# A fused recurrence and two-matmul kernel on one core: w's row on another queue, the columns' step earlier, three loads and four small steps reordered

## The chip, the cores and the metric

The kernel runs on one core of a Trainium2 chip. A core has five engines that run their own instruction streams and meet at semaphores: TensorE (PE, matrix products, with PEld for its weight loads), VectorE (DVE), ScalarE (ACT), GpSimd (POOL) and SyncE (SP, which here only issues transfers). Transfers between HBM and the on-chip memory run on 16 DMA engines that all queues share. The metric is the device time of one execution in microseconds (us); lower is better.

## The reference

There are two parts in a row. The first is a linear attention with a decayed state, for 4 batches, 8 heads, 768 tokens and a head size of 48:

```python
for t in range(S):
    cur = einsum('bhd,bhe->bhde', u[None] * kt, vt)
    y[:, :, t] = einsum('bhd,bhde->bhe', rt, state + cur)
    state = w[None, :, :, None] * state + einsum('bhd,bhe->bhde', kt, vt)
```

The second takes the 3072 tokens with 384 features each, and computes `h = x @ w_in` (384 x 2048), `g = max(0.01 * h, h)` and `g @ w_out` (2048 x 384). All inputs and the output are f32; inside, most operands are bf16.

## The kernel before

**Stages.** The 768 tokens of a batch are cut into 6 chunks of 128 tokens, so there are 24 stages: stage n is one chunk of one batch, and stages 0 to 3 are the first chunks of the four batches. Within a chunk the recurrence is turned into matrix products. Rows of r and k are scaled with powers of w around the chunk's middle (tables `qtab`, `ktab`), turned so that the head features lie on the partitions (`tp`), and multiplied to a 128 x 128 matrix per head, which is masked to its triangle (`at`) and multiplied with v. From stage 4 on the state from the chunk before is added (`st`). The result, turned, is `xT`. The second part takes it in groups of four stages: `w_in` products into `gT` (ScalarE applies the leaky step), then `w_out` products into `out_sb`.

**The order.** A text, `ORDER`, lists all steps by short names, and `run` (L844) goes through it. Each name adds instructions to one engine's stream. A step waits only for what it reads or overwrites (`Sched.add`, L72), but every engine works through its own steps strictly in the order of the text; a DMA is issued by the engine on which it is added, in its place in that stream. The eight PSUM banks are handed out in the order of the text as well (`take`, `give`).

**The names that matter here** (a number behind a name is the stage; q and k, or a and b, are halves):

- `w8`, `w`, `u8`, `u`: four small loads of w and u. `w8` brings w with heads on partitions, `w` brings its row (`w_row`, L807). `k0`, `r0` load stage 0 in f32, on the queues of ScalarE and SyncE (L249). `k1`, `r1`, `v1` and so on load 96 KB each (as bf16), `wi0` to `wi3` a quarter of `w_in`, `wo0` to `wo3` a quarter of `w_out`; all of these are issued by GpSimd (L268, L278, L282).
- `qk0`, `v0z`, `v0y`, `wlz`, `zr`: VectorE writes zeros into gaps of tiles. `v0z` does it for v of stages 0 to 3, `v0y` for stages 4 to 23 (L354, L815); `zr` also fills a gap of `w_head` (L359). `one`, `ones`, `id8`, `id`, `tri`, `exps` are constants that VectorE makes; `trow`, `tcol` are GpSimd's.
- `Cw` (L618): w into columns, on TensorE; `Wl` its logarithm, `E` the table for stage 0's turned tiles, `bc` w spread over partitions, `lnw` its logarithm, `qtab`, `ktab` the tables (L393), `W` the state's decay `wl` (L657).
- `wu8` (L403), `Cu` (L629), `C` (L645): the product w u into the two columns `wu`. `u16`, `U` (L409), `utab`: u spread over partitions.
- `c0q@`, `c0k@` (L485): stage 0's r and k as bf16 into `raw`. `P` (L437) scales r or k of a stage on VectorE, `T` (L491) turns it on TensorE, `t` (L507) copies it out; `X` (L452) is `prod`, the product q k of a stage 0 to 3, `D` (L578) its sums on TensorE, `Q` scales v with them (L459); from stage 4 on `q` is row sums on VectorE (L466 to L470) and `Q` a product on GpSimd (L477). `A` (L521) is the matrix product, `M` the mask (L559, L563), `Y` (L692) the sum into PSUM, `y` its copy, `K` and `S` the state (L604, L677).
- `G`, `J` the products with `w_in` (L758), `g`, `j` their copies (L769); `H`, `h` those with `w_out` (L782, L794). `F2`, `F4` are 2 or 4 matmuls on constants with no use for the result (L315).

The first of GpSimd's loads are issued in this order: r1, wi1, k1, k3, v3, v0, r3, v1, r2, k2, wi3, k5, r5, r4, wi2, v2, k4, v4, wi0, v5, wo3.

Of the kernel before, what the change touches and what calls it, by code (L numbers as in the profile page):

```python
# [6 lines left out]
ALU = mybir.AluOpType  # L7
AF = mybir.ActivationFunctionType
# [4 lines left out]
B, H, S, D = 4, 8, 768, 48  # L13
# [3 lines left out]
NST = B * NC  # L17
HD = H * D
E = 64
NP = H // 2  # L20
# [4 lines left out]
NB = B  # L25
TURNED, DIAG, CARRY, EXACT, RAW = 6, 4, 4, 1, 1
STRIPS = 8
SWAP = 12
ORDER = """
w8 qk0 k0 v0z one r0 trow ones v0y tcol wlz r1 id8 wi1 u8 zr table Cw Wl id E w bc lnw c0q@ T0q c0k@ tri u exps k1 T0k  # L30
u16 wu8 Cu t0q t0k qtab P1q F2 k3 v3 U A0 ktab T1q v0 t1q X0 C D0 P1k T1k t1k F4 M0b P3k M0a T3k K3 utab X1 A1 D1 Q0
Y0 t3k P0k r3 P3q v1 M1a T3q r2 y0 k2 K0 M1b Q1 P2q W G0.1 Y1 t3q X3 wi3 A3 y1 g0.1 S3 T2q D3 G1.1 g1.1 k5 t2q r5 r4
P2k T2k wi2 S0 v2 M3b t2k Q3 G0.3 g0.3 G1.3 k4 M3a Y3 P5k A2 y3 P4q T4q v4 wi0 T5k v5 wo3 t4q g1.3 G3.1 q5 t5k Q5 G3.3
g3.3 P5q r6 wo2 X2 g3.1 M2b wo1 G3.2 D2 Q2 G0.2 g0.2 T5q t5q K2 P4k T4k M2a t4k S2 G1.2 g3.2 q4 Q4 K1 S1 Y2 A5 A4 G1.0
y2 G2.1 M5a G0.0 G2.3 M4a M5b Y5 g0.0 y5 M4b Y4 y4 G2.2 g2.2 K4 J2.4 j2.4 k6 wo0 J2.1 J2.2 g1.0 g1.2 S4 k7 P6q q6 j2.1
P6k P7k G2.0 r7 q7 X6T J2.6 j2.6 J2.3 j2.3 k8 G3.0 J2.7 j2.7 k9 r9 j2.2 J2.5 P7q g3.0 g2.3 X7T J2.0 H1 h1 r8 g2.0 Q6
P9k j2.0 H0 j2.5 H3 Q7 P9q X9T A6 P8k q8 P8q X8T v6 A7 M6a v7 M7a g2.1 ts qtabs ktabs H2 h2 v9 v11 v10 M6b Y6 M7b tris
y6 Q8 Y7 y7 K5 r11 K6 S6 r10 k10 S5 v8 k11 k12 k14 K7 S7 q9 Q9 h0 h3 J3.0 j3.0 J3.1 j3.1 J3.2 j3.2 J3.3 j3.3 J3.4 j3.4
J3.5 j3.5 J3.6 j3.6 J3.7 j3.7 A8 A9 M8a M8b M9a M9b P10q P10k X10T P11q P11k X11T r12 r14 k13 r13 q10 Q10 q11 Q11 H4
h4 Y8 Y9 y8 y9 K8 K9 S8 S9 P12q P12k X12T P13q P13k X13T s8 s9 H5 h5 J4.0 j4.0 J4.1 j4.1 J4.2 j4.2 J4.3 j4.3 J4.4 j4.4  # L40
J4.5 j4.5 J4.6 j4.6 J4.7 j4.7 q12 q13 A10 A11 M10a M10b M11a M11b v12 v14 k15 r15 v13 v15 Q12 Q13 H6 h6 H7 h7 Y10 Y11
y10 y11 K10 K11 B6 M12a M12b M13a M13b S10 S11 P14q P14k X14T P15q P15k X15T s10 s11 q14 q15 J5.0 j5.0 J5.1 j5.1 k16
k18 r16 r18 k17 r17 Q14 Q15 J5.2 j5.2 J5.3 j5.3 J5.4 j5.4 J5.5 j5.5 J5.6 j5.6 J5.7 j5.7 H8 h8 H9 h9 Y12 Y13 y12 y13
K12 K13 B7 M14a M14b M15a M15b S12 S13 P16q P16k X16T P17q P17k X17T s12 s13 q16 q17 J6.0 j6.0 J6.1 j6.1 v16 v18 k19
r19 v17 v19 Q16 Q17 J6.2 j6.2 J6.3 j6.3 J6.4 j6.4 J6.5 j6.5 J6.6 j6.6 J6.7 j6.7 H10 h10 H11 h11 Y14 Y15 y14 y15 K14
K15 B8 M16a M16b M17a M17b S14 S15 P18q P18k X18T P19q P19k X19T s14 s15 q18 q19 J7.0 j7.0 J7.1 j7.1 k20 k22 r20 r22
k21 r21 Q18 Q19 J7.2 j7.2 J7.3 j7.3 J7.4 j7.4 J7.5 j7.5 J7.6 j7.6 J7.7 j7.7 H12 h12 H13 h13 Y16 Y17 y16 y17 K16 K17 B9
M18a M18b M19a M19b S16 S17 P20q P20k X20T P21q P21k X21T s16 s17 q20 q21 J8.0 j8.0 J8.1 j8.1 v20 v22 k23 r23 v21 v23
Q20 Q21 J8.2 j8.2 J8.3 j8.3 J8.4 j8.4 J8.5 j8.5 J8.6 j8.6 J8.7 j8.7 H14 h14 H15 h15 Y18 Y19 y18 y19 K18 K19 B10 M20a
M20b M21a M21b S18 S19 P22q P22k X22T P23q P23k X23T s18 s19 q22 q23 J9.0 j9.0 J9.1 j9.1 Q22 Q23 J9.2 j9.2 J9.3 j9.3  # L50
J9.4 j9.4 J9.5 j9.5 J9.6 j9.6 J9.7 j9.7 H16 h16 H17 h17 Y20 Y21 y20 y21 B11 M22a M22b M23a M23b J10.0 j10.0 J10.1
j10.1 J10.2 j10.2 J10.3 j10.3 J10.4 j10.4 J10.5 j10.5 J10.6 j10.6 J10.7 j10.7 H18 h18 Y22 Y23 y22 y23 H19 h19 J11.0
j11.0 J11.1 j11.1 J11.2 j11.2 J11.3 j11.3 J11.4 j11.4 J11.5 j11.5 J11.6 j11.6 J11.7 j11.7 H20 h20 H21 h21 H22 h22
"""


# [6 lines left out]
class Sched:  # L63
# [7 lines left out]

    def add(self, eng, emit, R=(), W=(), dma=None):  # L72
        o = Op()
        o.eng, o.emit, o.dma, o.inc, o.val = eng, emit, dma, False, None
        deps = []
        for key in R:
            w = self.writer.get(key)
            if w is not None:
                deps.append((w, True))
        for key in W:  # L80
            w = self.writer.get(key)
            if w is not None:
# [63 lines left out]
def bass_rwkv5_eagle__then__act_leaky_relu_kernel(  # L146
# [13 lines left out]
    def SB(name, shape, dt=BF16):  # L160
        return ctx.enter_context(nc.sbuf_tensor(name, shape, dt))
# [30 lines left out]
    ones = SB("ones", [128, 128])  # L192
# [10 lines left out]
    qk = [SB(f"qk{i}", [128, 2 * H, E]) for i in range(NQK)]  # L203
# [47 lines left out]
    def load_one(n, which, pace=()):  # L251
# [6 lines left out]
        if swapped(n):  # L258
# [5 lines left out]
            dst = both.rearrange("p n (h e) -> p (n h) e", h=H)[:, :, 0:D]  # L264
            add("pool", lambda: G.dma_start(dst, src), R=pace, W=[(which, n0, half), (which, n0 + 2, half)],
                dma=f"{which}{n}")
            return
        add("pool", lambda: G.dma_start(dst, src), R=pace, W=[(which, n)], dma=f"{which}{n}")  # L268

# [40 lines left out]
    def fill(n):  # L310
# [7 lines left out]

        add("pe", emit, R=["ones"], W=[("ps", i), f"fill{n}"])

# [32 lines left out]
    def zero_v(n0, n1):  # L353
        add("dve", lambda: V.memset(v_sb[:, n0:n1, :].rearrange("p n (h e) -> p (n h) e", e=E)[:, :, D:E], 0.0),  # L354
            W=[("v0", n) for n in range(n0, n1)])
# [66 lines left out]
    def hd(x):  # L422
        return x.rearrange("p (h d) -> p h d", d=D)

    def k_of(n):
        return k_sb[:, slot(n), :] if n >= EXACT else k_f[:, n, :]

    def r_of(n):
        return r_sb[:, slot(n), :] if n >= EXACT else r_f[:, n, :]

    def prep_half(n, half):
        iq = n % NQK
        src, tab, name, done = ((r_of(n), qtab, "r", "qp"), (k_of(n), ktab, "k", "kp"))[half]
        named = "qk"[half] + "tab"
        if swapped(n):
            tab, named = (qtab_s, ktab_s)[half], named + "_s"
        add("dve", lambda: V.tensor_tensor(qk[iq][:, H * half:H * half + H, 0:D], hd(src), hd(tab[:, :]), ALU.mult),  # L437
            R=loaded(name, n) + [named, ("qk0", iq)], W=[(done, iq)])

    def turn_dma(n):  # L440
        iq = n % NQK
# [203 lines left out]
    def decay_columns():  # L645
        ps_c, key = c_bank["u"]
        for hh in range(2):
            rows = slice(64 * hh, 64 * hh + D)
            add("dve", lambda rows=rows, hh=hh: V.tensor_copy(
                wu[rows, :, hh:hh + 1].rearrange("p m o -> p (m o)"), ps_c[rows, 0:NP]),  # L650
                R=[key, "wu"], W=[f"wu{hh}"])
        give(key)

# [134 lines left out]
    def g2_out(n, c0=0, c1=HD):  # L788
# [7 lines left out]
        if swapped(n):  # L796
# [7 lines left out]

    half_of = {"q": 0, "k": 1, "a": 0, "b": 1}
    single = {
        "w": lambda: add("sp", lambda: SP.dma_start(  # L807
            w_row[0:65:64, :], dram(w, 0, [[HD // 2, 2], [1, HD // 2]])),
            W=["w_row"], dma="w"),
        "w8": lambda: add("sp", lambda: SP.dma_start(w_head[:, :, 0:D], twice(w)), W=["w_head"], dma="w8"),  # L810
# [1 line left out]
        "u": lambda: add("sp", lambda: SP.dma_start(u_row[:, :], row(u)), W=["u_row"], dma="u"),  # L812
        "one": lambda: add("dve", lambda: V.memset(one_row[:, :], 1.0), W=["one_row"]),
        "tcol": tokens, "trow": token_rows, "ones": filled, "exps": exponents, "v0z": lambda: zero_v(0, NB),
        "v0y": lambda: zero_v(NB, NST), "zr": zero_raw, "qk0": zero_qk, "wlz": zero_w,  # L815
        "id": identity, "tri": triangle, "table": preload, "id8": small_identity, "wu8": wu_product,
        "bc": spread_w, "lnw": log_w, "qtab": lambda: table(qtab, tcol, "q", "tcol"),
        "ktab": lambda: table(ktab, kexp, "k", "kexp"), "Cw": w_columns, "Cu": wu_columns, "E": turned_table,
# [94 lines left out]
```

## Time and profile before

| | |
|---|---|
| median of 3 runs | 167.31 us (166.94 to 167.38) |
| the profiled execution | 166.78 us |
| its span, first to last instruction | 165.0 us |
| busy in the span | PE 157.4, PEld 119.7, DVE 105.5, ACT 90.4, POOL 109.5 us |
| transfers | 20.21 MB, 123 GB/s in the mean |

A profile is of one execution. Its times are microseconds from the span's start. In a timeline a row has the start, the length, the engine, the line, the operation with its tiles (out<-in), the number of instructions that the row merges, and in brackets how long the engine was idle before it and what ended the wait. In the chain of waits a row has the start, the length and what the end of the kernel waited for. In the view of transfers a row ends with the size and the median time from the start of an issue to the landing. In the table by stretches the columns are the stretch, its length, the busy time of PE, PEld, DVE, ACT and POOL, the granted clock, the DMA engines' share and GB/s. An "ACTq" or "SPq" is the engine's sequencer, which issues and waits. Matmuls are pipelined and their ends are modelled, so a busy PE isn't always PE at its peak.

### The profile page before, as it was taken

How to read it: one execution, taken by the hardware profiler on the slowest of the kernel's cores; microseconds unless marked ns; L12 is line 12 of the kernel's file. 1: busy time of each engine (PE TensorE's matmuls, PEld its weight loads, DVE VectorE, ACT ScalarE, POOL GpSimd, SP SyncE). 2: the span in 40 equal slices, each digit the busy share in tenths (PEclk: the TensorE clock that was granted, in tenths of full speed). 3: DMA queues.
4: the chain of work that ended last, by engine and by line, in shares of the span. 5: the costliest groups of instructions: out<-in, count | busy, mean ns of one | idle time of the engine just before them, and what ended most of it. 6: DMA issues, size and time to landing. Idle time of an engine off the chain costs nothing.

```text
span 165.0 us, 5331 instructions
## 1 busy us (share of the span) xinstructions
PE 157.4 (95%) x2303; PEld 119.7 (73%) x2303; DVE 105.5 (64%) x254; ACT 90.4 (55%) x170; POOL 109.5 (66%) x125
## 2 busy tenths in 40 slices
PE   0899999999999999999999999999999999999994
PEld 0487899985568678668668678678678668678663
DVE  7798998269378699948939939939939933000000
ACT  3856883865168339347447447438438439449121
POOL 8999798987999969999199399299380270000000
PEclk9999999999999999999999999999999999999999
DMA  7999999999999999999939959959980630020023
GB/s 110 149 141 158 169 189 190 181 150 154 149 153 202 121 118 137 158 208 130 160 90 113 145 134 94 163 132 81 104 192 4 127 97 3 4 61 34 17 82 97
DMA packets 101365, 20.21 MB, mean 123 GB/s; under 512 B 94555, under 2 KB 101342, under 8 KB 101342
## 3 DMA queue, kind: packets, MB, share of 16 engines
q0 software_dynamic: 76512, 10.03, 93.2%
q1 hardware_dynamic: 23790, 9.65, 29.8%
q8 instruction: 18, 0.29, 0.8%
q10 hardware_dynamic: 1040, 0.20, 0.6%
q14 instruction: 5, 0.04, 0.1%
HBM read 20.45 MB, written 4.72 MB: 153 GB/s over the span
## 4 chain that ended last, share of the span: by engine, by line
PE 91%; ACT 2%; DVE 2%; DMA 2%; SPq 1%; issue 0%; ACTq 0%
PE ps L782 38%; PE ps L758 37%; PE ps L719 6%; PE ps L529 2%; PE ps L500 2%; DMA w_row<-in_w_dram 2%; PE ps L548 1%; PE ps L595 1%; PE ps L604 1%; PE ps L315 1%; ACT xT L733 1%; DVE at L559 1%; PE ps L379 1%; DVE st L677 1%; PE ps L712 1%; ACT out_sb L794 0%
## 5 line engine op out<-in xcount | busy, mean ns | idle before, releaser
L758 PE MATMUL ps<-xT,w_in_sb 128*128 128x256 bf16 (+1 forms) x672 | 66.2, 257 | 0.2
L782 PE MATMUL ps<-w_out_sb,gT 128*128 128x384 bf16 (+2 forms) x400 | 64.6, 320 | 0.0
L769 ACT ACTIVATE gT<-ps 128x512 bf16<-128x512 f32 x96 | 56.3, 598 | 14.8 <-PE ps L758 10.9
L758 PEld LDWEIGHTS ps<-xT,w_in_sb 128*128 128x128 bf16 x672 | 57.2, 98 | 6.6 <-ACT xT L733 0.5
L477 POOL TENSOR_TENSOR at<-ident,s_tok 128x512 bf16<-128x512 bf16 x40 | 42.1, 1081 | 24.8 <-DVE s_tok L470 24.7
L782 PEld LDWEIGHTS ps<-w_out_sb,gT 128*128 128x128 bf16 x400 | 38.1, 98 | 23.1
L794 ACT ACTIVATE out_sb<-ps 128x384 f32<-128x384 f32 (+2 forms) x25 | 11.8, 478 | 45.3 <-PE ps L782 45.3
L563 DVE CAST_PREDICATED at<-mask,ps 128x512 bf16<-128x512 uint16 x28 | 17.8, 685 | 4.7 <-PE ps L529 4.6
L563 DVE CAST_PREDICATED at<-mask_s,ps 128x512 bf16<-128x512 uint16 x12 | 7.7, 687 | 16.1 <-PE ps L548 16.1
L268 POOL DMA_DIRECT2D v_sb<-in_v_dram x18 | 16.3, 920 | 0.0
L268 POOL DMA_DIRECT2D r_sb<-in_r_dram x17 | 15.7, 928 | 0.1
L268 POOL DMA_DIRECT2D k_sb<-in_k_dram x17 | 15.6, 924 | 0.0
L468 DVE TENSOR_TENSOR rku<-r_sb,ku 128x384 bf16<-128x384 bf16 x20 | 12.2, 611 | 0.7
L733 ACT ACTIVATE xT<-ps 128x384 bf16<-128x384 f32 x24 | 10.8, 491 | 2.7 <-PE ps L719 2.6
L470 DVE TENSOR_REDUCE s_tok<-rku 128x8 f32<-128x384 bf16 x20 | 11.1, 553 | 0.7
L719 PE MATMUL ps<-at,v_sb 128*32 128x128 bf16 x384 | 10.8, 223 | 0.0
L719 PEld LDWEIGHTS ps<-tp,st 128*32 128x32 bf16 x240 | 7.2, 96 | 3.0 <-issue 2.9
L719 PEld LDWEIGHTS ps<-at,v_sb 128*32 128x32 bf16 x384 | 8.8, 98 | 0.5 <-issue 0.2
L719 PE MATMUL ps<-tp,st 128*32 128x128 bf16 x240 | 9.1, 221 | 0.0
L671 DVE TENSOR_TENSOR sum_t<-ps,st 64x192 bf16<-64x192 f32 x24 | 8.5, 354 | 0.6
L466 DVE TENSOR_TENSOR ku<-k_sb,u_tab 128x384 bf16<-128x384 bf16 x20 | 7.0, 352 | 2.0 <-DMA k_sb<-in_k_dram 1.8
L437 DVE TENSOR_TENSOR qk<-k_sb,ktab 128x384 bf16<-128x384 bf16 x17 | 7.5, 443 | 1.1 <-DMA k_sb<-in_k_dram 1.0
(82 smaller groups left out, 119.9 us busy)
## 6 DMA issues: line engine op xcount, KB each, us to landing
out_dram<-out_sb SPq DMA_DIRECT2D x17, 192.0 KB, 3.3
v_sb<-in_v_dram POOLq DMA_DIRECT2D x24, 96.0 KB, 5.1
r_sb<-in_r_dram POOLq DMA_DIRECT2D x23, 96.0 KB, 4.5
k_sb<-in_k_dram POOLq DMA_DIRECT2D x23, 96.0 KB, 5.3
w_in_sb<-in_moe_w_in_dram POOLq DMA_DIRECT2D x4, 384.0 KB, 6.3
w_out_sb<-in_moe_w_out_dram POOLq DMA_DIRECT2D x4, 384.0 KB, 7.5
out_dram<-out_sb SPq DMA_DIRECT2D x12, 96.0 KB, 2.2
tp<-qk SPq DMA_TRANSPOSE x18, 4.5
```

The source lines that it names most:

```text
L268: add("pool", lambda: G.dma_start(dst, src), R=pace, W=[(which, n)], dma=f"{which}{n}")
L468: add("dve", lambda: V.tensor_tensor(rku[i2][:, :], r_of(n), ku[i2][:, :], ALU.mult), R=loaded("r", n) + [("ku", i2)], W=[("rku", i2)])
L470: add("dve", lambda: V.tensor_reduce(s_tok[i2][:, :], hd(rku[i2][:, :]), AX.X, ALU.add), R=[("rku", i2)], W=[("s", i2)])
L477: add("pool", lambda hh=hh, s_of=s_of: G.tensor_tensor(at[ia][:, hh, :, :], ident[:, :].unsqueeze(1).to_broadcast([128, NP, 128]), s_of.un ...
L563: add("dve", lambda: V.copy_predicated(at[n % NAT][:, hh, :, :], tri[:, :].bitcast(mybir.dt.uint16).unsqueeze(1).to_broadcast([128, NP, 12 ...
L671: add("dve", lambda part=part: V.tensor_tensor(both[part], kv[part[0]], st[n % NT][part], ALU.add), R=[key, ("st", n % NT)], W=[("sum", n ...
L719: last = PE.matmul(ps_y[32 * q:32 * q + 32, 128 * s:128 * s + 128], a, m, start=not whole and step == 0, stop=step == len(columns[q]) - 1)
L733: add("act", lambda: A.activation(xT[ix][:, :, 128 * slot:128 * slot + 128], ps_y[:, 0:HD].rearrange("p (s t) -> p s t", t=128), AF.Copy), ...
L758: last = PE.matmul(ps_g[:, step * f:step * f + step], w_in_sb[:, s, 128 * fb:128 * fb + 128], xT[ix][:, s, t], start=s == 0, stop=s == NSL ...
L769: add("act", lambda: A.activation(gT[ig][:, fb0:fb0 + count, t], ps_g[:, :].rearrange("p (f t) -> p f t", t=128 * width), AF.Prelu, alpha= ...
L782: last = PE.matmul(ps_o[:, 0:c1 - c0], gT[ig][:, s, 128 * slot:128 * slot + 128], w_out_sb[:, s, c0:c1], start=s == 0, stop=s == NFB - 1)
L794: add("act", lambda: A.activation(out_sb[io][:, c0:c1], ps_o[:, 0:c1 - c0], AF.Copy), R=[key], W=held)
```

## The change

The beginning of `ORDER` is rewritten, and four places in the code change.

- `w` is issued by ScalarE, right behind `k0`, instead of by SyncE.
- `zr` moves up to just behind `qk0`, `id8` ahead of `ones`, and `v0y` out of the opening. It is split: `v0y` is now stages 4 to 7, behind `P5q`, and the new `v0x` is stages 8 to 23, behind `g2.2`, ahead of `K4`.
- `tri` and `exps` come ahead of `id`; `wu8` goes behind `P1q` and `X0` ahead of `A0`; `F4` stands ahead of `A0` and `F2` behind `U`.
- `u16` goes behind `ktab`; `U` behind the turns of stage 1 (`T1k`, `t1k`).
- `Cu` goes behind `A0`, and `C` is done by ScalarE instead of VectorE.
- `wi1` goes from behind `r1` to behind `v0`, so that GpSimd's order begins r1, k1, k3, v3, v0, wi1, r3.
- `P0k` reads the bf16 copy in `raw` instead of the f32 tile.
- `W` goes from ahead of `G0.1` to behind `t3q`, and `S0` from ahead of `v2` to behind `M3a`.

```diff
-w8 qk0 k0 v0z one r0 trow ones v0y tcol wlz r1 id8 wi1 u8 zr table Cw Wl id E w bc lnw c0q@ T0q c0k@ tri u exps k1 T0k
-u16 wu8 Cu t0q t0k qtab P1q F2 k3 v3 U A0 ktab T1q v0 t1q X0 C D0 P1k T1k t1k F4 M0b P3k M0a T3k K3 utab X1 A1 D1 Q0
-Y0 t3k P0k r3 P3q v1 M1a T3q r2 y0 k2 K0 M1b Q1 P2q W G0.1 Y1 t3q X3 wi3 A3 y1 g0.1 S3 T2q D3 G1.1 g1.1 k5 t2q r5 r4
-P2k T2k wi2 S0 v2 M3b t2k Q3 G0.3 g0.3 G1.3 k4 M3a Y3 P5k A2 y3 P4q T4q v4 wi0 T5k v5 wo3 t4q g1.3 G3.1 q5 t5k Q5 G3.3
+w8 qk0 zr k0 w v0z one r0 trow tcol id8 ones wlz tri exps r1 u8 table Cw Wl id E bc lnw c0q@ T0q c0k@ u k1 T0k t0q t0k
+qtab ktab P1q wu8 X0 F4 k3 v3 A0 Cu u16 T1q v0 wi1 C t1q D0 P1k T1k t1k U F2 M0b P3k M0a T3k K3 utab X1 A1 D1 Q0 Y0
+t3k P0k r3 P3q v1 M1a T3q r2 y0 k2 K0 M1b Q1 P2q G0.1 Y1 t3q W X3 wi3 A3 y1 g0.1 S3 T2q D3 G1.1 g1.1 k5 t2q r5 r4 P2k
+T2k wi2 v2 M3b t2k Q3 G0.3 g0.3 G1.3 k4 M3a S0 Y3 P5k A2 y3 P4q T4q v4 wi0 T5k v5 wo3 t4q g1.3 G3.1 q5 t5k Q5 G3.3
...
+        src, reads = (raw[:, H * half:H * half + H, 0:D], [("raw", half)]) if n < RAW else (hd(src), loaded(name, n))
+        add("dve", lambda: V.tensor_tensor(qk[iq][:, H * half:H * half + H, 0:D], src, hd(tab[:, :]), ALU.mult),
+            R=reads + [named, ("qk0", iq)], W=[(done, iq)])
...
-            add("dve", lambda rows=rows, hh=hh: V.tensor_copy(
-                wu[rows, :, hh:hh + 1].rearrange("p m o -> p (m o)"), ps_c[rows, 0:NP]),
+            add("act", lambda rows=rows, hh=hh: A.activation(
+                wu[rows, :, hh:hh + 1].rearrange("p m o -> p (m o)"), ps_c[rows, 0:NP], AF.Copy),
...
-        "w": lambda: add("sp", lambda: SP.dma_start(
+        "w": lambda: add("act", lambda: A.dma_start(
...
-        "v0y": lambda: zero_v(NB, NST), "zr": zero_raw, "qk0": zero_qk, "wlz": zero_w,
+        "v0y": lambda: zero_v(NB, 2 * NB), "v0x": lambda: zero_v(2 * NB, NST), "zr": zero_raw, "qk0": zero_qk, "wlz": zero_w,
```

More of the change, by code (lines that the diff above doesn't have):

```diff
@@ L29 @@
 ORDER = """
-w8 qk0 k0 v0z one r0 trow ones v0y tcol wlz r1 id8 wi1 u8 zr table Cw Wl id E w bc lnw c0q@ T0q c0k@ tri u exps k1 T0k
-u16 wu8 Cu t0q t0k qtab P1q F2 k3 v3 U A0 ktab T1q v0 t1q X0 C D0 P1k T1k t1k F4 M0b P3k M0a T3k K3 utab X1 A1 D1 Q0
-Y0 t3k P0k r3 P3q v1 M1a T3q r2 y0 k2 K0 M1b Q1 P2q W G0.1 Y1 t3q X3 wi3 A3 y1 g0.1 S3 T2q D3 G1.1 g1.1 k5 t2q r5 r4
-P2k T2k wi2 S0 v2 M3b t2k Q3 G0.3 g0.3 G1.3 k4 M3a Y3 P5k A2 y3 P4q T4q v4 wi0 T5k v5 wo3 t4q g1.3 G3.1 q5 t5k Q5 G3.3
-g3.3 P5q r6 wo2 X2 g3.1 M2b wo1 G3.2 D2 Q2 G0.2 g0.2 T5q t5q K2 P4k T4k M2a t4k S2 G1.2 g3.2 q4 Q4 K1 S1 Y2 A5 A4 G1.0
@@ L35 @@
[L35 to L53, printed above, removed]
+w8 qk0 zr k0 w v0z one r0 trow tcol id8 ones wlz tri exps r1 u8 table Cw Wl id E bc lnw c0q@ T0q c0k@ u k1 T0k t0q t0k
@@ new lines @@
+qtab ktab P1q wu8 X0 F4 k3 v3 A0 Cu u16 T1q v0 wi1 C t1q D0 P1k T1k t1k U F2 M0b P3k M0a T3k K3 utab X1 A1 D1 Q0 Y0
+t3k P0k r3 P3q v1 M1a T3q r2 y0 k2 K0 M1b Q1 P2q G0.1 Y1 t3q W X3 wi3 A3 y1 g0.1 S3 T2q D3 G1.1 g1.1 k5 t2q r5 r4 P2k
+T2k wi2 v2 M3b t2k Q3 G0.3 g0.3 G1.3 k4 M3a S0 Y3 P5k A2 y3 P4q T4q v4 wi0 T5k v5 wo3 t4q g1.3 G3.1 q5 t5k Q5 G3.3
+g3.3 P5q v0y r6 wo2 X2 g3.1 M2b wo1 G3.2 D2 Q2 G0.2 g0.2 T5q t5q K2 P4k T4k M2a t4k S2 G1.2 g3.2 q4 Q4 K1 S1 Y2 A5 A4
+G1.0 y2 G2.1 M5a G0.0 G2.3 M4a M5b Y5 g0.0 y5 M4b Y4 y4 G2.2 g2.2 v0x K4 J2.4 j2.4 k6 wo0 J2.1 J2.2 g1.0 g1.2 S4 k7
@@ new lines @@
+P6q q6 j2.1 P6k P7k G2.0 r7 q7 X6T J2.6 j2.6 J2.3 j2.3 k8 G3.0 J2.7 j2.7 k9 r9 j2.2 J2.5 P7q g3.0 g2.3 X7T J2.0 H1 h1
+r8 g2.0 Q6 P9k j2.0 H0 j2.5 H3 Q7 P9q X9T A6 P8k q8 P8q X8T v6 A7 M6a v7 M7a g2.1 ts qtabs ktabs H2 h2 v9 v11 v10 M6b
+Y6 M7b tris y6 Q8 Y7 y7 K5 r11 K6 S6 r10 k10 S5 v8 k11 k12 k14 K7 S7 q9 Q9 h0 h3 J3.0 j3.0 J3.1 j3.1 J3.2 j3.2 J3.3
+j3.3 J3.4 j3.4 J3.5 j3.5 J3.6 j3.6 J3.7 j3.7 A8 A9 M8a M8b M9a M9b P10q P10k X10T P11q P11k X11T r12 r14 k13 r13 q10
+Q10 q11 Q11 H4 h4 Y8 Y9 y8 y9 K8 K9 S8 S9 P12q P12k X12T P13q P13k X13T s8 s9 H5 h5 J4.0 j4.0 J4.1 j4.1 J4.2 j4.2 J4.3
@@ new lines @@
+j4.3 J4.4 j4.4 J4.5 j4.5 J4.6 j4.6 J4.7 j4.7 q12 q13 A10 A11 M10a M10b M11a M11b v12 v14 k15 r15 v13 v15 Q12 Q13 H6 h6
+H7 h7 Y10 Y11 y10 y11 K10 K11 B6 M12a M12b M13a M13b S10 S11 P14q P14k X14T P15q P15k X15T s10 s11 q14 q15 J5.0 j5.0
+J5.1 j5.1 k16 k18 r16 r18 k17 r17 Q14 Q15 J5.2 j5.2 J5.3 j5.3 J5.4 j5.4 J5.5 j5.5 J5.6 j5.6 J5.7 j5.7 H8 h8 H9 h9 Y12
+Y13 y12 y13 K12 K13 B7 M14a M14b M15a M15b S12 S13 P16q P16k X16T P17q P17k X17T s12 s13 q16 q17 J6.0 j6.0 J6.1 j6.1
+v16 v18 k19 r19 v17 v19 Q16 Q17 J6.2 j6.2 J6.3 j6.3 J6.4 j6.4 J6.5 j6.5 J6.6 j6.6 J6.7 j6.7 H10 h10 H11 h11 Y14 Y15
@@ new lines @@
+y14 y15 K14 K15 B8 M16a M16b M17a M17b S14 S15 P18q P18k X18T P19q P19k X19T s14 s15 q18 q19 J7.0 j7.0 J7.1 j7.1 k20
+k22 r20 r22 k21 r21 Q18 Q19 J7.2 j7.2 J7.3 j7.3 J7.4 j7.4 J7.5 j7.5 J7.6 j7.6 J7.7 j7.7 H12 h12 H13 h13 Y16 Y17 y16
+y17 K16 K17 B9 M18a M18b M19a M19b S16 S17 P20q P20k X20T P21q P21k X21T s16 s17 q20 q21 J8.0 j8.0 J8.1 j8.1 v20 v22
+k23 r23 v21 v23 Q20 Q21 J8.2 j8.2 J8.3 j8.3 J8.4 j8.4 J8.5 j8.5 J8.6 j8.6 J8.7 j8.7 H14 h14 H15 h15 Y18 Y19 y18 y19
+K18 K19 B10 M20a M20b M21a M21b S18 S19 P22q P22k X22T P23q P23k X23T s18 s19 q22 q23 J9.0 j9.0 J9.1 j9.1 Q22 Q23 J9.2
@@ L54 @@
+j9.2 J9.3 j9.3 J9.4 j9.4 J9.5 j9.5 J9.6 j9.6 J9.7 j9.7 H16 h16 H17 h17 Y20 Y21 y20 y21 B11 M22a M22b M23a M23b J10.0
+j10.0 J10.1 j10.1 J10.2 j10.2 J10.3 j10.3 J10.4 j10.4 J10.5 j10.5 J10.6 j10.6 J10.7 j10.7 H18 h18 Y22 Y23 y22 y23 H19
+h19 J11.0 j11.0 J11.1 j11.1 J11.2 j11.2 J11.3 j11.3 J11.4 j11.4 J11.5 j11.5 J11.6 j11.6 J11.7 j11.7 H20 h20 H21 h21
+H22 h22
 """
@@ L436, in prep_half @@
             tab, named = (qtab_s, ktab_s)[half], named + "_s"
-        add("dve", lambda: V.tensor_tensor(qk[iq][:, H * half:H * half + H, 0:D], hd(src), hd(tab[:, :]), ALU.mult),
-            R=loaded(name, n) + [named, ("qk0", iq)], W=[(done, iq)])
+        src, reads = (raw[:, H * half:H * half + H, 0:D], [("raw", half)]) if n < RAW else (hd(src), loaded(name, n))
+        add("dve", lambda: V.tensor_tensor(qk[iq][:, H * half:H * half + H, 0:D], src, hd(tab[:, :]), ALU.mult),
+            R=reads + [named, ("qk0", iq)], W=[(done, iq)])
     def turn_dma(n):
```

## The prediction

> **What bounds the kernel now.** I read the page first (busy times, then the shares of the chain), then the chain of waits in order of time, then each engine's timeline of the first 31 us, and last the transfers.
>
> ```profile
> PE 157.4 (95%) x2303; PEld 119.7 (73%) x2303; DVE 105.5 (64%) x254; ACT 90.4 (55%) x170; POOL 109.5 (66%) x125
> ...
> PE 91%; ACT 2%; DVE 2%; DMA 2%; SPq 1%; issue 0%; ACTq 0%
> ```
>
> TensorE (PE) works 157.4 of 165.0 us and holds 91% of the chain. Only 7.6 us are idle, so a change to the opening can give a microsecond or so, and only if nothing else holds TensorE afterwards. Where the chain leaves TensorE is seen in its rows (start, length, what):
>
> ```profile
> 2.17 2.90 DMA w_row<-in_w_dram
> ...
> 15.04 0.42 DVE prod L452
> ...
> 16.20 0.47 DVE st L677
> ...
> 17.73 0.61 DVE at L559
> ...
> 18.38 0.34 PE ps L712 x3
> ```
>
> The row of w lands at 2.17 + 2.90 = 5.07. From about 15 to 18.3 VectorE leads, until the second mask of stage 3 (17.73) lets Y3 start at 18.38. After that TensorE is on the chain nearly to the end. Every edit aims at these two places. But the chain names one releaser at each step, and there is a second limit just behind it. VectorE's timeline after 18 us (start, length):
>
> ```profile
> 18.24 0.35 DVE L437 TENSOR_TENSOR qk<-k_sb,ktab 128x384 bf16<-128x384 bf16 x1
> 18.68 0.36 DVE L437 TENSOR_TENSOR qk<-r_sb,qtab 128x384 bf16<-128x384 bf16 x1
> ...
> 20.47 1.27 DVE L452 TENSOR_TENSOR prod<-tp 128x512 bf16<-128x512 bf16 x1
> ```
>
> The second row is P4q, which reads r of stage 4. The row before it ends at 18.59, and P4q starts 0.09 later. GpSimd's timeline has the issues of the loads, and the view of transfers has, for five narrow stretches, the time from an issue's start to landing (in this order: r1, wi1, v0, r4, and one late load):
>
> ```profile
> 1.41 1.07 POOL L268 DMA_DIRECT2D r_sb<-in_r_dram  x1
> 2.47 0.77 POOL L278 DMA_DIRECT2D w_in_sb<-in_moe_w_in_dram  x1
> 3.20 0.94 POOL L268 DMA_DIRECT2D k_sb<-in_k_dram  x1
> ...
> 5.95 0.88 POOL L268 DMA_DIRECT2D v_sb<-in_v_dram  x1
> ...
> 12.80 0.92 POOL L268 DMA_DIRECT2D r_sb<-in_r_dram  x1
> ...
> 20.37 2.27 POOL L477 TENSOR_TENSOR at<-ident,s_tok 128x512 bf16<-128x512 bf16 x2 [0.86 <-DVE s_tok L470]
> ```
>
> ```profile
> r_sb<-in_r_dram POOLq DMA_DIRECT2D x1, 96.0 KB, 4.0
> w_in_sb<-in_moe_w_in_dram POOLq DMA_DIRECT2D x1, 384.0 KB, 5.6
> v_sb<-in_v_dram POOLq DMA_DIRECT2D x1, 96.0 KB, 4.9
> r_sb<-in_r_dram POOLq DMA_DIRECT2D x1, 96.0 KB, 5.9
> k_sb<-in_k_dram POOLq DMA_DIRECT2D x1, 96.0 KB, 3.7
> ```
>
> So r1 lands at 1.41 + 4.0 = 5.4, wi1 (the first quarter of w_in that is loaded) at 2.47 + 5.6 = 8.1, v0 at 5.95 + 4.9 = 10.85, and r4 at 12.80 + 5.9 = 18.7. P4q starts at 18.68, that is, on the landing of r4. What hangs on it runs in line on VectorE: the row sums of stage 5, GpSimd's product at 20.37, prod of stage 2 at 20.47, which ends at 21.74; TensorE's D2 reads it:
>
> ```profile
> 21.88 0.24 PE L578 MATMUL ps<-wu,prod 128*128 128x2 bf16 x4
> ```
>
> That is 0.14 after prod's end, in the middle of TensorE's unbroken stretch. **The stretch from 18.7 to 21.9 therefore hangs on a load, and a shorter opening leaves it where it is.**
>
> The loads themselves are worked off in order. Their rate, in two stretches (last column GB/s): 8 to 12 us, when many issues wait, and 113 to 117 us, when GpSimd issues one load after another into an empty queue:
>
> ```profile
> 8.00:12.00 4.00, 4.00 (x41) 3.03 (x40) 3.91 (x12) 2.53 (x5) 4.00 (x6) 1.00 2.67 141
> 113.00:117.00 4.00, 4.00 (x36) 3.36 (x35) 3.81 (x14) 3.65 (x7) 2.91 (x4) 1.00 2.04 108
> ```
>
> A load of 96 KB (98,304 B) takes 0.70 us at 141 GB/s and 0.91 us at 108. The 3.7 above is from that second stretch: the landing time without a backlog. v0's 4.9 and r4's 5.9 contain a queue.
>
> **The change part by part.**
>
> *w on ScalarE's queue.* The load of k0, behind which w now stands, in the timeline and in the view of transfers:
>
> ```profile
> 0.73 0.41 ACTq L249 DMA_DIRECT2D k_f<-in_k_dram  x1
> ```
>
> ```profile
> k_f<-in_k_dram ACTq DMA_DIRECT2D x1, 192.0 KB, 3.0
> ```
>
> SyncE issues w at 2.17. On ScalarE it is issued at 1.14, and k0 lands at 0.73 + 3.0 = 3.7, so w lands between there and the old 5.07; I take 3.9, near k0. One more issue, about 0.4 us, stands on ScalarE before its table load, which is over before the columns come. If that cover went, the columns would be late by as much, still ahead of before.
>
> *Columns sooner; zeroing later.* These rows carry it:
>
> ```profile
> 4.24 0.38 PE L623 MATMUL ps<-ident,w_head 8*64 8x4 f32 x4 [4.24 <-DVE w_head L359]
> ```
>
> ```profile
> 2.47 1.12 DVE L354 MEMSET v_sb<- 128x1280 uint32 x1 [0.22 <-issue]
> ...
> 30.16 0.56 DVE L680 TENSOR_TENSOR sum_t<-ps,st 128x384 bf16<-128x384 f32 x1 [1.73 <-PE ps L604]
> ```
>
> The columns' matmuls waited for VectorE, which had the 1.12 us of zeroing in front. Without it, and with the small identity earlier, they start near 2.9: 1.3 sooner, so the turned table too. The zeroing comes back in two parts. Sixteen stages (1.12 x 16/20 = 0.9 us) go ahead of S4, where VectorE sits idle 1.73 us: hidden; without that idle time 0.9 would show. Four stages (0.22) go between P5q and prod of stage 2, thus on the path found above. But prod takes 1.27 us there and 0.42 at 15.04: it stands from 20.47 behind GpSimd's first product, which began at 20.37. A prod that starts 0.22 later still ends with it. I take 0, the other end being rival D.
>
> The Trainium skill, "SBUF — State Buffer", section "Who interferes with whom", says that a VectorE instruction with two SBUF inputs waits for a GpSimd one that reads SBUF, and one with at most one SBUF input, outside certain fast modes, does not. By that rule prod waits and a memset does not, which speaks against D; no row shows a memset beside a GpSimd product.
>
> *Spread of u, fillers, decay columns, P0k.* U, F2 and F4 change places with the same six filler matmuls; F4 now fills TensorE's wait for VectorE's t0k. The two casts of wu go from VectorE to ScalarE, and P0k reads the bf16 copy in raw instead of f32. All lie before stage 4; I take 0 at the end of that stretch, since the load decides it. From below they are part of the lead in rival C.
>
> *W behind t3q, S0 behind the masks of stage 3.*
>
> ```profile
> 13.65 0.73 ACT L657 ACTIVATE wl<-wcol 48x192 bf16<-48x192 f32 x2
> ```
>
> W leaves 0.6 to 0.7 us ahead of t3q, of which S3, which needs W, takes some back; S0 leaves 0.47. With the earlier start Y3 could come 1.1 us sooner. S0 is now ahead of P5k and P4q, in VectorE's wait for r4, so it costs nothing.
>
> *w_in's first quarter behind v0.* This is the part that costs. Today wi1 (8.1 - 5.4 = 2.7 us of transfer) stands second; meanwhile GpSimd issues ahead, and the queue never runs dry. Now k1 is issued at 2.47, and v0 at 2.47 + (5.95 - 3.20) = 5.22. Each of k1, k3, v3, v0 comes into a queue that is done with the one before (0.91 of issue against 0.70 of transfer), so v0 lands at 5.22 + 3.7 = 8.9, and wi1, with its 2.7, at 11.6. The same set was complete at 10.85. So all loads from r3 on land later: +0.7 by these landings, +0.84 by rates (4 x 0.21), 0 if no gap opens. I take 0.65, on the landings' side, as they are read to a tenth. v0 lands 2 sooner, but VectorE then meets r3, the first of the later ones, and the lead is spent before stage 4.
>
> Sum: r4 lands at 19.35, P4q starts there (+0.65), prod ends at 22.4, D2 starts at 22.45 to 22.5 instead of 21.88: **+0.6**. TensorE has no later idle time to give it back. The profiled execution took 166.78 (span 165.0 and 1.8 around it): 167.4. The median of the runs, 167.31, lies 0.53 above it: **167.9**.
>
> **The rivals.**
>
> B, *the queue has no gap*: the issues overlap enough for the engines, and loads land as before. Then P4q stays on r4's landing, at most 0.1 to 0.2 is won before D2: 167.2. For it: landings differ between engines and only the last is seen. Against it: 108 GB/s when issues come one at a time.
>
> The Trainium skill, "DMA: Bandwidth & Descriptors", section "Anatomy of one DMA — SWDGE (gpsimd) path", fits a load to 2.0 us plus bytes over 436 GB/s. By it 96 KB would be 2.2 us, no backlog would ever form, and the order would be free, as in B; the trace differs, with 3.7 without a queue and 4.9 and 5.9 with one.
>
> C, *the opening passes through*: faster. The chain of waits says so literally: w's landing and VectorE's chain lead, and both are cut by about 1.1: 166.2. It decides if r4 lands at 17.6 or sooner, or if the 0.09 ahead of P4q is not r4's doing. Against it: only the order of the loads ahead of r3 changes, and what stands ahead of r4 is the same.
>
> D, *zeroing on the path*: the memset of four stages waits for GpSimd's product as prod does, and prod then waits for the second one, 1.1 longer (2.27 for two): 169.0.
>
> That w behind k0's 192 KB lands no sooner than 5.07 would change nothing: the opening has about 1 us to spare ahead of r4. It is inside B and the forecast.
>
> **How the numbers follow.** Forecast 0.58 (its own range 167.6 to 168.2, from a gap of 0.3 to 0.85), B 0.19, C 0.16, D 0.07. A measurement here can tell about 0.3% (0.5 us: 166.8, 167.8) from no change. Faster is C, 0.16; same is B and the forecast's low end, 0.19 + 0.10 = 0.29; slower is the rest, 0.55. The range that holds 8 in 10 takes in the forecast, B and the edges of the others: 166.9 to 168.4.
>
> **What would show it.** Right: the columns' matmuls near 2.9, w_row landing near 3.9, v0 near 8.9, wi1 past 11, r4 past 19.2; VectorE idle about 1 us ahead of P4q; prod of stage 2 ending near 22.4; D2 near 22.5 and the rest shifted alike. Wrong: r4 at 18.7 or less (B), Y3 and D2 both about a microsecond sooner (C), or a memset of over 1 us at 21 (D). A wait of TensorE in a place that had none, from another order of its banks, would make the whole sum wrong.

## The result and the profile after

The median of the kernel after is 167.84 us, that of the kernel before, run beside it, 166.93. The ratio is **1.0044, 95% interval 1.0028 to 1.0060**: slower by 0.7 us (0.0044 x 166.93). (The two medians lie 0.91 apart; the ratio and its interval are what the text goes by.) The profiled execution of after took 167.55 us with a span of 165.7; before it was 166.78 and 165.0.

**The page of after**, busy times and the chain's shares:

```profile
PE 158.7 (96%) x2303; PEld 120.7 (73%) x2303; DVE 105.2 (63%) x253; ACT 90.9 (55%) x172; POOL 109.5 (66%) x125
...
PE 90%; DMA 4%; POOL 4%; ACT 1%; issue 0%; DVE 0%; POOLq 0%; ACTq 0%
```

The DMA share is 4% now and was 2%, and POOL, which issues the loads, has 4% where it was not listed. VectorE's 2% have become 0%, and SyncE's queue is no longer listed. (Lines of the code are 1 or 2 higher in after.)

**The opening**, TensorE's timeline of after and then ScalarE's:

```profile
2.48 0.38 PE L625 MATMUL ps<-ident,w_head 8*64 8x4 f32 x4 [2.48 <-DVE ones L306]
4.28 1.01 PE L380 MATMUL ps<-w_row,one_row 1*128 1x192 f32 x4 [1.42 <-DMA w_row<-in_w_dram]
```

```profile
0.74 0.43 ACTq L250 DMA_DIRECT2D k_f<-in_k_dram  x1
1.21 1.06 ACTq L809 DMA_DIRECT2D w_row<-in_w_dram  x1
2.29 1.28 ACT L309 ACT_TABLE_LOAD   x1 [2.29 <-issue]
3.59 0.17 ACT L644 ACTIVATE wcol<-ps 128x4 f32<-128x4 f32 x1
```

The columns start at 2.48 instead of 4.24, and w is spread (L380) from 4.28 instead of from 5.1. So the opening did become shorter, by 1.8 and 0.8 us. At stage 0's turns on TensorE 0.7 of it is left (they start at 5.36, were 6.06): VectorE's cast of r0 waits for that load and starts at 4.65, as in before (4.66). ScalarE's issue of w takes 1.06 us, and the table load behind it ends at 2.29 + 1.28 = 3.57, 0.7 after the columns' matmuls (2.48 + 0.38 = 2.86); ScalarE takes the columns at 3.59.

**The loads**, GpSimd's issues in after, then (view of transfers) the landings of v0, wi1 and r4:

```profile
2.46 1.79 POOL L269 DMA_DIRECT2D k_sb<-in_k_dram  x2
4.23 1.82 POOL L269 DMA_DIRECT2D v_sb<-in_v_dram  x2
6.03 0.76 POOL L279 DMA_DIRECT2D w_in_sb<-in_moe_w_in_dram  x1
...
11.93 1.79 POOL L269 DMA_DIRECT2D r_sb<-in_r_dram  x2
```

```profile
v_sb<-in_v_dram POOLq DMA_DIRECT2D x1, 96.0 KB, 3.5
...
w_in_sb<-in_moe_w_in_dram POOLq DMA_DIRECT2D x1, 384.0 KB, 5.9
...
r_sb<-in_r_dram POOLq DMA_DIRECT2D x1, 96.0 KB, 6.8
```

v0, the second load of its row, is issued at 5.09 and lands 3.5 later, at 8.60 (before 10.85). wi1 lands at 6.03 + 5.9 = 11.9 (before 8.1). r4, also the second of its row, is issued at 12.79 (before 12.80) and lands at 19.6 instead of 18.7. The same three microseconds in before and in after, in the table by stretches (last column GB/s), show why:

```profile
5.00:8.00 3.00, 2.88 (x19) 1.73 (x19) 2.21 (x8) 3.00 (x8) 3.00 (x5) 1.00 1.65 163
```

```profile
5.00:8.00 3.00, 2.75 (x24) 1.67 (x22) 2.49 (x7) 2.40 (x6) 3.00 (x5) 1.00 2.25 116
```

163 GB/s became 116, though GpSimd issues in both without a pause (POOL 3.00 of 3.00): with the small loads first, the transfers wait for the issues. v0's time from issue to landing says the same: it was 4.9 us and is 3.5, and a load with no queue in front takes about as long (3.7 late in before).

**What hangs on them**, the chain of waits of after and then VectorE's timeline:

```profile
6.76 5.94 DMA r_sb<-in_r_dram
12.70 0.02 issue
12.72 0.37 DVE qk L439
13.09 0.05 issue
13.14 0.61 PE ps L502 x4
...
20.71 2.01 PE ps L760 x36
22.72 0.08 issue
22.80 0.24 PE ps L580 x4
```

```profile
12.72 0.36 DVE L439 TENSOR_TENSOR qk<-r_sb,qtab 128x384 bf16<-128x384 bf16 x1 [1.43 <-DMA r_sb<-in_r_dram]
...
19.59 0.36 DVE L439 TENSOR_TENSOR qk<-r_sb,qtab 128x384 bf16<-128x384 bf16 x1 [0.41 <-DMA r_sb<-in_r_dram]
...
21.47 0.27 DVE L355 MEMSET v_sb<- 128x256 uint32 x1
21.66 0.99 DVE L454 TENSOR_TENSOR prod<-tp 128x512 bf16<-128x512 bf16 x1
```

The lead of the opening ends at 12.7, where VectorE waits 1.43 us for r3. P4q waits for r4 and starts 0.91 later than before (19.59, was 18.68); prod ends at 22.65 (21.74); D2 starts at 22.80 (21.88): **+0.92**. The last copy into `out_sb` starts 0.87 later (163.44, was 162.57).

The chain shows one more thing: from 13.14 to 22.72 it stays on TensorE, whose own work ends 0.07 after prod. Two limits stand level there. In the same products with `w_in` (TensorE's timelines, before and then after) is the reason:

```profile
13.81 0.84 PE L758 MATMUL ps<-xT,w_in_sb 128*128 128x128 bf16 x12
```

```profile
13.87 1.48 PE L760 MATMUL ps<-xT,w_in_sb 128*128 128x128 bf16 x12
15.14 0.53 PE L714 MATMUL ps<-ident,vs 128*128 128x128 bf16 x3
...
19.16 0.33 PE L714 MATMUL ps<-ident,vs 128*128 128x128 bf16 x3
```

The twelve matmuls start at the same time and take 1.48 instead of 0.84 us, and three others take 0.53 at 15.14 but 0.33 at 19.16. TensorE works at a slower rate at first and changes to the full one at about 16.4 us here and about 13.3 in before; the granted clock shows 1.00 in both. So this profile alone can't say which of the two made D2 late, and the experiments had to tell two theories apart. **L, the loads:** small loads in front leave the queue unfilled, and all that follow land later. **K, the fillers:** the new places of `F2` and `F4` bring the full rate later, and TensorE's own work is what is late. Two of the kernels below, c3 and d3, were profiled in an execution 2.1 to 2.2 us longer than their medians; nothing is read from those profiles, and their rows have dashes.

### The profile page after: what moved, and what is told of

It reads as the page before. It is cut to its first block, busy times and chain, and to the rows that moved or that the text cites. A ratio compares the mean times of both kernels' runs of the same rounds, so it can differ in the third digit from the quotient of the medians.

```text
span 165.7 us, 5331 instructions
## 1 busy us (share of the span) xinstructions
PE 158.7 (96%) x2303; PEld 120.7 (73%) x2303; DVE 105.2 (63%) x253; ACT 90.9 (55%) x172; POOL 109.5 (66%) x125
## 4 chain that ended last, share of the span: by engine, by line
PE 90%; DMA 4%; POOL 4%; ACT 1%; issue 0%; DVE 0%; POOLq 0%; ACTq 0%
PE ps L760 39%; PE ps L784 38%; PE ps L721 6%; DMA r_sb<-in_r_dram 4%; PE ps L531 2%; PE ps L550 1%; PE ps L502 1%; POOL v_sb L269 1%; POOL k_sb L269 1%; PE ps L597 1%; PE ps L606 1%; POOL r_sb L269 1%; ACT xT L735 1%; ACT out_sb L796 0%; POOL w_in_sb L279 0%; PE ps L714 0%
## 5 line engine op out<-in xcount | busy, mean ns | idle before, releaser
L760 PEld LDWEIGHTS ps<-xT,w_in_sb 128*128 128x128 bf16 x672 | 57.8, 99 | 6.4 <-ACT xT L735 0.3
```

What stands on the lines that cost most here:

```text
L760: last = PE.matmul(ps_g[:, step * f:step * f + step], w_in_sb[:, s, 128 * fb:128 * fb + 128], xT[ix][:, s, t], start=s == 0, stop=s == NSL ...
```

## The experiments

Each kernel is compared with the kernel before on the same chip (medians there 167.31, 167.38 and 167.43 for the groups a and b, c, and d; the first two rows are the pair of the result). "GB/s" is that of the stretch from 5 to 8 us. "Rate" is the time at which TensorE's matmuls reach the short spacing, read from its timeline; r4's landing and D2's start are from the profiles.

| kernel | ratio to before, 95% | median us | GB/s | r4 landed | rate | D2 |
|---|---|---|---|---|---|---|
| before (profile) | 1 | 166.93 | 163 | 18.65 | 13.3 | 21.88 |
| after (profile) | 1.0044 (1.0028 to 1.0060) | 167.84 | 116 | 19.57 | 16.4 | 22.80 |
| a1, after, wi1 second again | 0.9987 (0.9960 to 1.0015) | 167.17 | 164 | 18.36 | 15.1 | 21.96 |
| b1, before, wi1 behind v0 | 1.0023 (0.9990 to 1.0056) | 167.84 | 112 | 19.00 | 11.9 | 22.22 |
| a2, after with more fillers | 1.0033 (0.9997 to 1.0069) | 168.32 | 109 | 20.11 | 15.2 | 23.33 |
| a3, a1 with r4 and wi0 sooner | 0.9987 (0.9959 to 1.0014) | 166.96 | 162 | 18.41 | 16.7 | 23.02 |
| c1, after, F2 and F4 exchanged | 1.0040 (1.0014 to 1.0066) | 168.25 | 114 | 19.51 | 16.2 | 22.74 |
| c2, a3, F2 and F4 exchanged | 1.0003 (0.9977 to 1.0029) | 167.46 | 161 | 17.51 | 15.4 | 22.70 |
| c3, before, r4 and wi0 sooner | 0.9965 (0.9935 to 0.9995) | 167.18 | - | - | - | - |
| c4, before, F2 and F4 exchanged | 0.9998 (0.9971 to 1.0026) | 167.52 | 157 | 19.57 | 16.0 | 22.80 |
| d1, c3 again | 0.9982 (0.9955 to 1.0008) | 167.04 | 160 | 18.05 | 12.4 | 21.67 |
| d2, before, wi1 behind k3 | 1.0017 (0.9990 to 1.0045) | 167.52 | 133 | 18.69 | 12.5 | 21.91 |
| d3, before without the fillers | 1.0008 (0.9977 to 1.0039) | 167.60 | - | - | - | - |
| d4, d1 with W and S0 later | 0.9973 (0.9940 to 1.0006) | 166.80 | 164 | 17.51 | 14.1 | 22.00 |

**a1: all of the change but wi1.** Against after:

```diff
-exps r1 u8 table
+exps r1 wi1 u8 table
...
-T1q v0 wi1 C t1q
+T1q v0 C t1q
```

> The changed kernel with the first quarter of w_in (wi1) loaded second again, right behind r1; all else as changed. Theory L (loads): the queue of loads has no gap any more, r4 lands near 18.7 us instead of 19.6, P4q of VectorE starts there, and the time is that of the kernel before or up to 0.3 us less (ratio 0.998 to 1.001). Theory K (clock): in the changed kernel TensorE came to its full rate 3 us later (its 12 matmuls of 128 columns at 13.9 us took 1.48 us instead of 0.84), since the fillers and the opening's order are others; this kernel has the same fillers, so the late rate and 0.5 to 0.9 us more than before stay (ratio 1.003 to 1.006).

0.9987 (0.9960 to 1.0015): the loss is gone, and r4 lands at 18.36. But the shorter opening, which a1 keeps, gains nothing that can be told. Where its lead goes stands in the chain of waits of a1:

```profile
3.19 5.45 DMA k_sb<-in_k_dram
...
8.74 0.37 DVE qk L438
...
22.12 0.08 PE ps L579 x4
```

k1, behind wi1, lands at 8.64, about as in before (8.82), and TensorE's work runs on from there. In after k1 lands at 6.08, and the chain meets r3 at 12.70 instead. With either order the lead runs into a load. The rates of the loads, in the table by stretches of a1 and then of b1, the next kernel, differ as those of before and after do:

```profile
5.00:8.00 3.00, 2.82 (x26) 1.71 (x24) 2.43 (x7) 2.46 (x6) 3.00 (x5) 1.00 1.65 164
```

```profile
5.00:8.00 3.00, 2.89 (x19) 1.37 (x17) 2.36 (x8) 3.00 (x8) 3.00 (x5) 1.00 2.16 112
```

**b1: wi1 alone.** Against before:

```diff
-r1 id8 wi1 u8 zr
+r1 id8 u8 zr
...
-T1q v0 t1q X0
+T1q v0 wi1 t1q X0
```

> The kernel before with one edit: wi1 is loaded behind v0. Theory L: v0 lands near 8.7 us, r4 near 19.5, P4q starts there, and the whole loss is here: 0.6 to 0.9 us more than before (ratio 1.004 to 1.006). Theory K: the fillers stand where they stood, the full rate comes as before (matmuls of 128 columns at the fast spacing from 13 to 14 us on), and the time is within 0.2 us of before.

1.0023 (0.9990 to 1.0056): below the 1.004 to 1.006 expected, and the sign by itself is not certain. The profile is clear on the path. Its chain of waits names the prediction's second limit outright:

```profile
12.78 6.21 DMA r_sb<-in_r_dram
19.00 0.02 issue
19.02 0.04 DVE qk L437
...
20.62 0.26 DVE qk L437
20.89 1.20 DVE prod L452
22.08 0.14 issue
22.22 0.24 PE ps L578 x4
```

r4's landing, VectorE's line, prod, D2; and TensorE has its full rate at 11.9 here, sooner than before. D2 is 0.34 later than before with no part of theory K in play. That is about half of the 0.6 of the prediction. v0 lands at 9.60 here, not near 8.7 as expected, and in a2 and c1 at 10.38 and 9.56: only in after does each of the four small loads land as into an empty queue.

**a2: more fillers.** Against after:

```diff
-id E bc lnw
+id E F6 bc lnw
...
-X0 F4 k3
+X0 F4 F1 k3
...
-Q0 Y0 t3k
+Q0 Y0 F3 t3k
```

> The changed kernel with ten more filler matmuls on constants, in TensorE's idle places: six ahead of bc (which waits for w's row), one behind F4, three between Y0 and T3q. Their results are not used. Theory K: TensorE comes to its full rate sooner, and the time goes back towards before (ratio 0.998 to 1.002). Theory L: r4 still lands near 19.5, P4q starts there, and the time stays 0.6 to 0.9 us above before, whatever the rate of the opening's matmuls.

1.0033 (0.9997 to 1.0069): nothing is seen to come back. The full rate is at 15.2, and P4q still waits for r4, in VectorE's timeline of a2:

```profile
20.13 0.36 DVE L438 TENSOR_TENSOR qk<-r_sb,qtab 128x384 bf16<-128x384 bf16 x1 [1.28 <-DMA r_sb<-in_r_dram]
```

**a3: the loads better than before.** Against a1:

```diff
-k5 t2q r5 r4 P2k
+k5 r4 t2q r5 P2k
...
-k4 M3a S0
+k4 wi0 M3a S0
...
-v4 wi0 T5k
+v4 T5k
```

> The changed kernel with the loads ordered for what waits for them: wi1 second again, r4 directly behind k5 and ahead of r5, wi0 directly behind k4 and ahead of v4. Theory L: r4 lands 0.4 to 0.7 us sooner than before (near 18.1), P4q and what hangs on it follow, wi0 lands near 24.5, and the lead of the opening gets through in part: 0.2 to 0.7 us less than before (ratio 0.996 to 0.999). Theory K: as a1_wi1_back, 0.5 to 0.9 us more than before.

0.9987 (0.9959 to 1.0014): no gain that can be told. In its profile r4 lands at 18.41, yet P4q starts only at 19.55, without a wait for a load; TensorE (full rate at 16.7) is what is late, and D2 follows its own products at 23.02. That execution is bound there by TensorE's own work, and sooner loads are worth nothing in it.

**c1, c2 and c4: the fillers exchanged**, in after, in a3 and in before (the diff is c1's; in c4 the two are exchanged the other way):

```diff
-P1q wu8 X0 F4 k3 v3
+P1q wu8 X0 F2 k3 v3
...
-t1k U F2 M0b
+t1k U F4 M0b
```

> The changed kernel with the two groups of fillers exchanged: two ahead of A0 (near 7 us) and four behind U (near 10 us), where the kernel before has four; wi1 stays behind v0. Two theories that both hold a part: L, r4's landing holds P4q; K, TensorE's full rate comes later because the dense fillers left the stretch from 8.5 to 13 us. K: the full rate (12 matmuls of G0.1 in 0.84 us, not 1.48) is there by 14.5 us, and the changed kernel's loss shrinks by 0.2 to 0.4 us. L alone: r4 still lands past 19, P4q starts on it, 0.4 to 0.7 us above before in both cases.

> As c1_swap, and the loads ordered as in a3_loads (wi1 second, r4 ahead of r5, wi0 ahead of v4): both limits are taken away. L and K together: the lead of the opening gets through, 0.4 to 0.9 us less than before (ratio 0.995 to 0.998), P4q near 18, D2 near 21.2. If only L held, as a3_loads (ratio 0.9987). If neither is the cause: no change against a3_loads and D2 near 22.

> The kernel before with the two groups of fillers exchanged (four behind P1q near 7.3 us, two behind the turns of stage 1 near 10 us), nothing else. K: the full rate comes later than 13.3 us (at about 15 or 16), TensorE reaches D2 late, and the time rises by 0.2 to 0.6 us with more scatter. L: the loads are as before, r4 near 18.7, no change (within 0.1 us).

c1 is at 1.0040 (1.0014 to 1.0066), where after is. c4, before with the fillers in after's order, is at 0.9998 (0.9971 to 1.0026). c2 misses the gain expected of it: 1.0003 (0.9977 to 1.0029). The fillers' places change nothing in the time that can be told, and **theory K falls** as far as it lays the loss on them. (What a late rate costs by itself, these kernels don't show: the rate was late in all three profiles.) c4's profile (TensorE's timeline) is also a warning:

```profile
14.37 1.48 PE L758 MATMUL ps<-xT,w_in_sb 128*128 128x128 bf16 x12
```

Here the slow rate lasts to 16.0, r4 lands as late as in after, and the time is before's. One profiled execution is one sample, for the rate and for the landings.

**c3 and d1: before with r4 ahead of r5 and wi0 ahead of v4** (the moves of r4 and wi0 shown for a3), one kernel in two groups:

> The kernel before with r4 loaded ahead of r5 and wi0 ahead of v4, nothing else. L: r4 lands near 18.1 instead of 18.7, but VectorE ends P5k at 18.6 only, so P4q gains 0.1 and the time 0 to 0.2 us: the opening's own chain is the next limit. K: the full rate as before, no change.

> The kernel before with r4 ahead of r5 and wi0 ahead of v4, a second time, beside the other three on one chip. Theory L says that the loads' order sets the time of the opening: again 0.2 to 0.7 us less than before (ratio 0.996 to 0.999). If the first result was scatter: within 0.1% of before.

0.9965 (0.9935 to 0.9995) and 0.9982 (0.9955 to 1.0008). Both are below 1; the second alone doesn't exclude no change, and the first gained more than the 0 to 0.2 us expected of it. In d1 P4q no longer waits for r4, and D2 starts at 21.67, 0.21 sooner than before.

**d2: wi1 halfway.** Against before, wi1 goes behind k1 and k3:

```diff
-r1 id8 wi1 u8 zr
+r1 id8 u8 zr
...
-F2 k3 v3
+F2 k3 wi1 v3
```

> The kernel before with wi1 behind k1 and k3, so with two small loads ahead of it instead of four (or none). Theory L, with a gap for each small load that comes into an empty queue: half the loss, 0.3 to 0.5 us more than before (ratio 1.002 to 1.003), wi1 landing 0.4 us later than two loads of 0.7 us explain. If the loss comes from wi1's own lateness for G0.1: none, since it lands near 9.8, long ahead of 13.8.

1.0017 (0.9990 to 1.0045): between the two orders, and not to be told from either. Its rate of the loads, 133 GB/s, lies between them too.

**d3: before without its fillers** (`F2` and `F4` struck out). It leaves out six matmuls whose results nobody reads.

> The kernel before without its six filler matmuls. Theory K (fillers bring TensorE's full rate sooner): the full rate comes later than in any profile so far and the time rises by 0.3 to 0.8 us. Against it (the rate's coming differs from execution to execution whatever the fillers, and the loads set the time): within 0.2% of before.

1.0008 (0.9977 to 1.0039): the six fillers are worth nothing here that this measurement can tell.

**d4: d1 with W and S0 later**, W where the change has it and S0 still later, behind P5q. Against d1:

```diff
-P2q W G0.1 Y1 t3q X3
+P2q G0.1 Y1 t3q W X3
...
-wi2 S0 v2
+wi2 v2
...
-P5q r6
+P5q S0 r6
```

> d1_loads_again with two edits of the change on the chain from 13.8 to 18.7 us: W behind t3q, and S0 behind P5q, where VectorE's prod waits for GpSimd anyway. Theory L: with r4 early the chain is the next limit, so this is 0.2 to 0.5 us under d1_loads_again, 0.5 to 1.0 us under before (ratio 0.994 to 0.997). If TensorE's own work at the slow rate is the next limit instead: no better than d1_loads_again.

0.9973 (0.9940 to 1.0006), median 166.80, the lowest of the kernels tried, but just outside the expected 0.994 to 0.997. As the interval reaches 1, it isn't shown to beat the kernel before. In its profile r4 lands at 17.51 and prod ends at 21.50, but D2 starts at 22.00, behind TensorE's own products.

**Together.** The four kernels with wi1 behind v0 have ratios of 1.0023 to 1.0044, mean 1.0035 (0.6 us). The three with wi1 second and r4 where it was (a1, c4, d3) have 0.9987 to 1.0008, mean 0.9998. The five with r4 and wi0 sooner (a3, c2, c3, d1, d4) have 0.9965 to 1.0003, mean 0.9982. r4 lands at 19.0 to 20.1 (mean 19.55) in the four, at 18.65, 18.36 and 19.57 (mean 18.86) in before, a1 and c4: 0.7 later. No order of the fillers sorts the kernels in this way.

Three things in the profiles bear theory L out, link by link. The rate of the loads sorts them without overlap: 109 to 116 GB/s with wi1 behind v0, 157 to 164 with wi1 second. The six loads r1, wi1, k1, k3, v3 and v0 are all in at 11.53 to 12.27 (mean 11.96) in the four and at 10.66 to 11.71 (mean 11.18) in the seven with wi1 second: 0.8 later. And in all seven profiles in which r4 lands at 18.65 or later, D2 starts 3.22 to 3.23 us after that landing, whatever the fillers and the rate. In the five with r4 in by 18.41, D2 follows TensorE's own products instead, 3.6 to 5.2 after r4. Theory L holds.

## Why the prediction was right

- **The mechanism** was the one forecast: the lead of the opening is spent at r3, r4 lands later, and P4q, the row sums, GpSimd's product, prod and D2 follow it one by one. a1 takes the whole loss away with one name moved, and b1's chain shows the limit that in before was only inferred. What the forecast had no term for is TensorE's own slower work, which in the profile of after stood level with it (22.72 against prod's end at 22.65); that the loads make the loss is known from the other kernels, not from that profile.
- **The loads' size:** +0.65 was forecast. The profile has +0.92 for r4, over the upper bound of 0.84, but the difference of the means over the profiles, +0.7, is the better figure, as r4's landing differs by up to 1.2 between profiles with the same loads in front of it. v0 at 8.9 was 8.60, wi1 at 11.6 was 11.89. The times agree: 0.6 forecast, 0.7 measured. That the median came within 0.1 of the 167.9 is in part luck: the forecast put it 0.53 above the profiled execution, from three runs of before; beside after, the median of before was only 0.15 above its profiled execution, and after's 0.29.
- **Columns** at 2.9 came at 2.48, as the smaller identity was ready sooner. **w_row** at 3.9 came at 4.24, as ScalarE's issue of w took 1.06 us and not the 0.4 taken for it. Here the cover failed that the prediction named: the table load was not over before the columns came, and they waited 0.7 us for it. They were still ahead of before (ScalarE took them at 3.59, was 4.66), as it said, and what was lost of the lead costs nothing, since the lead ends at a load.
- **The zeroing** cost nothing, as taken. The part of 16 stages ran in VectorE's idle time, 0.91 us at 29.50. The part of 4 stages took 0.27 at 21.47, though GpSimd had its product in hand from 21.29, and prod ended 0.28 after the first product. Rival D falls. By the Trainium skill, "SBUF — State Buffer", section "Who interferes with whom", a memset isn't held up there and prod is. Both rows agree (0.27 us for the memset, the same as for that size in the opening; 0.99 for prod, which took 0.42 without such a neighbour).
- **W and S0 later** were to let Y3 start as much as 1.1 sooner. It started 0.78 later (19.16, was 18.38). This step failed in the profiled execution: the prediction took TensorE's rate to be as in before, without saying so, and the slow rate lasted until 16.4. So VectorE's idle time ahead of P4q, about 1 us in the forecast, was 0.41. In d4 the two moves bring nothing that can be told.
- **Rival B** (no gap) fails on the 116 GB/s and on a1; **rival C** (the opening passes through) on the waits for r3 and, in a1, for k1.

**What stays open** is why TensorE's full rate comes when it does. All six profiles with the changed opening have it at 15.1 to 16.7; five of the six with the opening of before have it at 11.9 to 14.1, and c4 at 16.0. It may be the opening or the execution; with one profile of each it can't be settled. It doesn't sort after from a1, as both have it late. But where r4 is in by 18.41, a later rate goes with a later D2 (21.67 with the rate at 12.4 in d1, 23.02 with 16.7 in a3), so it may be part of why the shorter opening gains nothing in a1; no run here settles that.

## What to carry to other kernels

A row of small loads in front of a large one can empty a queue that the large one would have kept filled; count the issue time against the transfer time of each before moving one. A chain of waits names one limit, so look for the next landing that a shortened stretch will run into. And when a change is worth half a per cent, judge it by ratios of many executions of several kernels that share the part, and use one profile only to see the mechanism.

## What was not expected of the hardware

- **TensorE's rate.** Its matmuls start at 2.5 to 4.3 us and reach the full rate at 11.9 to 16.7. The Trainium skill, "TensorE: Matmul & The Clock Gate", section "What's actually happening", gives about 3.4 us of sustained work. In a2, whose matmuls follow one another almost without a gap from 2.8 us on, it took until 15.2. The measurement decides here. Two rows of a2's timeline, most of the second still at the slow spacing (the next twelve such matmuls, at 16.59, take 0.84):

```profile
6.19 1.27 PE L315 MATMUL ps<-ones 128*128 128x256 bf16 x5
...
14.18 1.31 PE L759 MATMUL ps<-xT,w_in_sb 128*128 128x128 bf16 x12
```

- **A small issue can be long.** w's 1.5 KB took ScalarE 1.06 us to issue behind another load; the 192 KB of k0 ahead of it took 0.43.
- **The first load can land later for the one behind it.** r1 lands at 5.1 to 5.5 us when small loads follow it, and at 5.4 to 6.7 when wi1 does, though it is issued at the same time.
